# A fused linear attention and two mixtures of experts on one core: the first attention steps in another order, their evictions on VectorE, other planned load times, and early expert results kept in the input tile

## The chip, the cores and the metric

The kernel runs on one core of one Trainium2 chip. The metric is the device time of one execution in microseconds (us). Before the change it is 1239.43 us, the median of three runs (1235.06 to 1243.83).

## What is computed

Attention is a recurrence over 768 tokens for 4 batches of 8 heads with 48 elements each: a 48x48 state per head is read by the query, then corrected by the key and the value.

```python
for t in range(S):
    kt, vt, bt = (k_n[:, :, t], v[:, :, t], beta[:, :, t, None])
    y[:, :, t] = np.einsum('bhd,bhde->bhe', q[:, :, t], state)
    v_old = np.einsum('bhde,bhd->bhe', state, kt)
    state = state + bt[:, :, :, None] * np.einsum('bhd,bhe->bhde', kt, vt - v_old)
```

`k_n` is the key divided by its length. The 3072 rows of 384 elements then pass a first mixture (8 experts, each row to the one with the highest logit, `relu(x @ w1) @ w2`, times two gates) and a second one (4 experts, every row through all, weighted by `domain_probs`).

## The kernel before

**Three phases.** The attention with the routing of its rows (`Attention`, `Router`), the first mixture (`Moe.moe1`) and the second one (`Moe.moe2`) follow each other. Each phase is a list of operations with an engine, an assumed duration, what they read and write, and a priority; `Plan.order` (lines 132 to 188) plays the list through once, always taking the earliest operation that can start and among several the one of the lower priority number, and emits the program in that order. On the chip each engine then keeps strictly to its own order. Assumed durations therefore decide the order, not the time. A DMA is two planned operations: its issue on a queue (`D` is SyncE, `A` ScalarE, `G` GpSimd) and a transfer of `xfer` ns. Where TensorE (PE) has a planned gap, small matmuls of zeros (line 252) are put in.

**Attention.** The tokens of a batch are cut into 12 stages of 64. For each stage `st`: `load` (line 310) fetches keys, queries and values into `kf`, `qf` and `v` (5, 2 and 2 buffers); `keys` (319) transposes them on PE into a bank `pb` and moves that ("evicts" it) to `kqT`; `gram` (333) multiplies keys with keys and queries into `GQ` and collects diagonal blocks in `Dg`; `masks` (350) zeroes a triangle of `GQ` on GpSimd (POOL); `scale` (404) multiplies `v` by the key lengths `nt` on POOL. For each pair of stages `inverse` (359) inverts 16x16 triangles on VectorE (DVE): a transpose to `GZ`, a square root on ScalarE (ACT) into `s1`, small steps that give `nt`, then 29 dependent multiply and add steps on `X` (lines 374 to 376). `turn` (377) transposes `X` to `TN` and `C`, and `finish` (381) completes `C` by two PE products (`prod`, line 398) for each stage. `chain` (410) is the recurrence: `r` (values minus what the state gives), two triangular PE products `tri` into `rw` with an eviction to `w` after each, `up` into `Sp`, and the evictions of `Sp` to the state `Sf`, which the next stage needs.

**Routing and the early window.** `Router.done` routes 128 rows at a time; when 16 of the 24 row groups are placed, `early` (586) counts (`few`), gathers the first rows of experts 0 and 1 through one tile, splits and transposes them into `xe[0]` and `xe[1]`. `window(0)` (612) runs 192 rows of expert 0 while the attention ends: eight products into `h` (lines 624 to 626) and three into `y` (633 to 635), whose results go to `x2` in DRAM. Its tiles `h` and `y` lie in `GQ` buffers that the attention no longer needs. `moe1` begins with `window_` for expert 1 on `xe[1]` (line 815) and with the gathers `xg` of the other rows (802). Its tiles lie where the attention's were, so their first writers wait for what still reads there.

## Time and profile before

| what | before |
|---|---|
| median of three runs | 1239.43 us |
| the profiled execution's own time | 1235.26 us |
| its span, first to last instruction | 1233.7 us |
| busy: PE, DVE, ACT, POOL | 94%, 63%, 50%, 52% of the span |
| attention, up to the first product of `moe1` | 306.1 us |

A row of the trace's order of time gives start (us), duration (us), engine, line, operation, what is written from what, and the count; in brackets stands how long the engine had been idle before, and what released it. PEld is the weight load of a matmul, SPq, ACTq and POOLq are DMA issues. PEclk is the clock that the throttle granted to PE, as a share of 2.4 GHz.

### The profile page before, as it was taken

The page shows a single profiled execution, that of the slowest core. Times are in us where ns is not written, and L with a number is a line of the kernel's source. Part 1 is how long each engine was busy: PE and PEld are TensorE (multiplying, and loading weights), DVE is VectorE, ACT ScalarE, POOL GpSimd, SP SyncE. Part 2 cuts the span into 40 slices and gives each one's busy share as a digit, 9 for nine tenths or more (in the row PEclk, how much of TensorE's full clock was granted, in tenths as well). Part 3 has the DMA queues.
Part 4 walks back from the last instruction along what each step waited for, and adds up shares of the span by engine and source line. Part 5 has one row for each costly group of instructions (what it writes and reads, how often), then busy time and mean ns, then how long its engine had stood idle before and what let it go on. Part 6 is the DMA issues. An engine that isn't in the chain of part 4 may idle for free.

```text
span 1233.7 us, 38757 instructions
## 1 busy us (share of the span) xinstructions
PE 1163.3 (94%) x16595; PEld 1018.3 (83%) x16595; DVE 778.2 (63%) x1583; ACT 619.2 (50%) x1129; POOL 642.0 (52%) x896
## 2 busy tenths in 40 slices
PE   6877888879899999999999999999999999999997
PEld 5876777768765555699999999999999999999997
DVE  3766647664578887166666556676666775555555
ACT  4646665553366666255454444454444554444442
POOL 9733422442573341075556544576544575566665
PEclk9989899989999999999999999999999999999999
DMA  8545442322499996111111111121111110111101
GB/s 136 90 98 119 97 92 58 94 83 69 93 263 240 251 231 199 39 38 40 40 39 40 36 44 44 48 60 51 46 57 49 52 40 27 40 53 52 53 27 40
DMA packets 151458, 100.74 MB, mean 82 GB/s; under 512 B 107697, under 2 KB 140433, under 8 KB 151281
## 3 DMA queue, kind: packets, MB, share of 16 engines
q1 hardware_dynamic: 133520, 69.18, 22.9%
q0 software_dynamic: 9216, 23.50, 6.7%
q10 hardware_dynamic: 8544, 5.53, 1.5%
q8 instruction: 131, 2.15, 0.7%
q14 instruction: 47, 0.38, 0.1%
HBM read 77.09 MB, written 15.77 MB: 75 GB/s over the span
## 4 chain that ended last, share of the span: by engine, by line
PE 57%; DVE 0%; issue 0%; POOL 0%; ACT 0%; POOLq 0%
PE b L956 31%; PE b L975 26%; POOL out_dram L994 0%; DVE h L968 0%; DVE cc L986 0%; DVE wa L990 0%; DVE sm L986 0%; ACT h L967 0%; ACT a L958 0%; POOLq L1052 0%; POOL sep L993 0%; POOLq L994 0%
## 5 line engine op out<-in xcount | busy, mean ns | idle before, releaser
L956 PE MATMUL b<-wb,v 128*128 128x256 f16 x3456 | 392.6, 273 | 0.7 <-PEq L923 0.7
L956 PEld LDWEIGHTS <-v 128*128 128x128 f16 x3456 | 336.7, 98 | 38.1 <-issue 1.1
L975 PE MATMUL b<-v,h 128*128 128x192 f16 x4032 | 348.0, 246 | 0.0
L975 PEld LDWEIGHTS <-h 128*128 128x128 f16 x4032 | 335.5, 98 | 2.2
L964 POOL TENSOR_TENSOR S<-a 128x256 f32<-128x256 f32 x192 | 150.8, 805 | 250.5 <-ACT a L958 250.2
L968 DVE TENSOR_TENSOR h<-a,h 128x768 f16<-128x768 f32 x96 | 133.0, 1386 | 133.2 <-ACT h L967 124.9
L968 DVE TENSOR_TENSOR h<-S,h 128x1024 f16<-128x1024 f32 x96 | 117.6, 1225 | 125.7 <-ACT h L967 125.7
L958 ACT ACTIVATE a<-b 128x512 f32<-128x512 f32 x192 | 113.8, 595 | 151.6 <-PE b L956 149.2
L967 ACT ACTIVATE h<-S 128x1024 f16<-128x1024 f32 x96 | 101.4, 1056 | 161.2 <-POOL S L964 141.5
L964 POOL TENSOR_TENSOR S<-S,a 128x256 f32<-128x256 f32 x96 | 127.0, 1323 | 0.0
L967 ACT ACTIVATE h<-a 128x768 f16<-128x768 f32 x96 | 81.0, 843 | 3.0
L964 POOL TENSOR_TENSOR S<-a,S 128x256 f32<-128x256 f32 x96 | 77.1, 803 | 7.2
L986 DVE TENSOR_TENSOR cc<-b,sm 128x192 f32<-128x192 f32 x192 | 58.7, 347 | 2.4 <-ACT sm L980 2.4
L833 POOL DMA_DIRECT2D x<-y x24 | 17.1, 712 | 61.5 <-DVE y L830 40.3
L818 DVE SCALAR_TENSOR_TENSOR h<-b,h 128x432 f16<-128x432 f32 (+2 forms) x72 | 37.8, 527 | 16.3 <-ACT h L817 16.2
L817 ACT ACTIVATE h<-b 128x432 f16<-128x432 f32 (+2 forms) x72 | 32.9, 466 | 29.5 <-PE b L815 29.0
L986 DVE TENSOR_TENSOR sm<-b,sm 128x192 f32<-128x192 f32 x144 | 46.2, 349 | 1.5
L767 DVE SCALAR_TENSOR_TENSOR v<-s,v 128x512 f16<-128x512 f32 (+2 forms) x56 | 42.6, 775 | 5.9 <-ACT v L766 5.8
L802 POOL DMA_INDIRECT xg<-xd,wid x28 | 30.5, 1088 | 22.8 <-issue 6.6
L269 POOL DMA_DIRECT2D stw<-in_moe_w_dram x28 | 16.0, 572 | 47.8 <-DVE X L376 17.9
L815 PE MATMUL b<-xt,w 128*128 128x432 f16 x216 | 40.2, 346 | 0.2 <-DVE h L818 0.2
L827 PE MATMUL b<-h,w 128*128 128x432 f16 x216 | 39.9, 346 | 0.0
(286 smaller groups left out, 1727.9 us busy)
## 6 DMA issues: line engine op xcount, KB each, us to landing
wb<-x SPq DMA_DIRECT2D x72, 256.0 KB
s<-in_moe_w_dram SPq DMA_DIRECT2D x40, 384.0 KB
s<-in_moe_w_dram SPq DMA_DIRECT2D x18, 512.0 KB
s<-in_moe_w_dram SPq DMA_DIRECT2D x24, 256.0 KB
xd<-ys ACTq DMA_DIRECT2D x24, 192.0 KB
x<-y POOLq DMA_DIRECT2D x18, 216.0 KB
stw<-in_moe_w_dram POOLq DMA_DIRECT2D x12, 256.0 KB
stw<-in_moe_w_dram POOLq DMA_DIRECT2D x16, 192.0 KB
```

The source lines that it names most:

```text
L767: self.op('V',(150+1.042*n)*self.slow,lambda: self.nc.vector.scalar_tensor_tensor(out=lo,in0=s,scalar=64.0,in1=hi,op0=ALU.mult,op1=ALU.sub ...
L815: nc.tensor.matmul(out=ps,lhsT=w1[:,a,k,f*128:(f+1)*128],rhs=xt[:,b*KD+k],start=i==0,stop=i==8); i+=1
L817: self.op('A',160+.85*n,lambda ps=ps,h=h: nc.scalar.activation(out=h[:,0],in_=ps,func=AF.Relu),[('p1',pi)],[('h',hi,0)],**U)
L818: self.op('V',150+1.042*n,lambda ps=ps,h=h: nc.vector.scalar_tensor_tensor(out=h[:,1],in0=ps,scalar=0.0,in1=h[:,0],op0=ALU.max,op1=ALU.sub ...
L827: nc.tensor.matmul(out=ps,lhsT=w2[:,a,f,d*128:(d+1)*128],rhs=hs[f][0][:,b],start=(f,i)==(0,0),stop=(f,i)==(KF-1,2))
L956: for c,y in PASS: nc.tensor.matmul(out=F[k][:,f],lhsT=w[:,c,d,c_:c_+128],rhs=self.xk[B%2][d][:,y,256*i:256*i+256],start=(f,z)==(0,0),stop ...
L958: self.op('A',620,lambda k=k,g=g: A.activation(out=a[ja][:,g].rearrange("p x t -> p (x t)"),in_=F[k].rearrange("p a t -> p (a t)"),func=AF ...
L964: self.op('G',930,lambda o=o,x=x,y=y,w=w: G.tensor_tensor(out=X[o],in0=X[x],in1=X[y],op=w),ka,[ks])
L967: self.op('A',200+.833*m,lambda h=h,q=q,g=g: A.activation(out=h[:,0,:,q],in_=g,func=AF.Copy),kg,[kh+(0,)])
L968: self.op('V',1400 if m==768 else 1350,lambda h=h,q=q,g=g: V.tensor_tensor(out=h[:,1,:,q],in0=g,in1=h[:,0,:,q],op=ALU.subtract),kg+[kh+(0, ...
L975: for z,(c,d) in enumerate(PASS): nc.tensor.matmul(out=Q[k][:,o,0:192],lhsT=h[:,c,g,x],rhs=w[:,d,m,y],start=(m,o,z)==(0,0,0),stop=(m,z)==( ...
L986: self.op('V',340,lambda o=o,k=k,y=y,x=x: V.tensor_tensor(out=o,in0=Q[k][:,y,0:192],in1=s[:,x],op=ALU.add),[(qk,k),('sm',z,x)],[ko])
```

## The change

Eight edits, all but the last two in the first stages of the attention.

1. The load of the square root's table onto ACT and the memset ahead of it move from priority -40 to -61, to the front of both engines.
2. `xfer` of a key, query or value load is 9.4 ns a row for stages 0 and 1, 12 for stages 2 to 4 (`LDX`), and 8.5 as before for the rest.
3. All key evictions of stages 0 and 1 go to DVE (before: one half of the heads on ACT).
4. Of the two evictions of a `gram` of stages 0 and 1 the second goes to DVE.
5. `masks` of stages 0 and 1 get a much earlier priority; those of stage 2 wait for the first state `Sf`.
6. `scale` of stage 0 is gone: `r` of stage 0 is one DVE multiplication of `v` by `nt` (before: a POOL multiplication, then an ACT copy). `scale` of stage 1 waits for `C` of stage 1, that of stage 2 for the first `Sf`.
7. In `window`, `y` is written over `xe`, the window's own input tile, after its last reader.
8. The three DMAs of `y` to `x2` go to SyncE's queue (`YQ`).

```diff
+LDX = 12
+YQ = 'D'
...
-        self.op('V',100,lambda: nc.vector.memset(self.s1,1.0),(),['s1'],"table")
-        self.op('A',1450,lambda: nc.scalar.activation(out=self.s1,in_=self.s1,func=AF.Sqrt),['s1'],['s1'],"table")
+        self.op('V',100,lambda: nc.vector.memset(self.s1,1.0),(),['s1'],"table",prio=-61)
+        self.op('A',1450,lambda: nc.scalar.activation(out=self.s1,in_=self.s1,func=AF.Sqrt),['s1'],['s1'],"table",prio=-61)
...
-                self.dma(d,h[b,:,64*st+x:64*st+x+m].rearrange("h t d -> t h d"),(),[(n,i,b,x)],f"ld {st} {w}",xfer=8.5*m,occ=640 if x in (0,64) and m==64 or x==0 else 490,q=q[b//2%len(q)])
+                self.dma(d,h[b,:,64*st+x:64*st+x+m].rearrange("h t d -> t h d"),(),[(n,i,b,x)],f"ld {st} {w}",xfer=(9.4 if st<2 else LDX if st<5 else 8.5)*m,occ=640 if x in (0,64) and m==64 or x==0 else 490,q=q[b//2%len(q)])
...
-            e='AV'[hh] if st<2 else 'A'; s=lambda P=P: P[0:112,:].rearrange("p (h g t) -> p h g t",h=4,g=2)
+            e='V' if st<2 else 'A'; s=lambda P=P: P[0:112,:].rearrange("p (h g t) -> p h g t",h=4,g=2)
...
-            for t in range(2): self.act(594,GQ[t][:,4*hh:4*hh+4].rearrange("p h i -> p (h i)"),lambda P=P[t]: P[:,:],[ks[t]],[wr[t]],tg,give=[ks[t]])
+            for t in range(2):
+                o=GQ[t][:,4*hh:4*hh+4].rearrange("p h i -> p (h i)")
+                if st<2 and t: self.op('V',690,lambda o=o,P=P[t]: nc.vector.tensor_copy(out=o,in_=P[:,:]),[ks[t]],[wr[t]],tg,give=[ks[t]])
+                else: self.act(594,o,lambda P=P[t]: P[:,:],[ks[t]],[wr[t]],tg,give=[ks[t]])
...
-            self.op('G',1250,lambda P=P,t=t: nc.gpsimd.tensor_tensor(out=P,in0=P,in1=self.mask[t].rearrange("p (o i) -> p o i",o=1).to_broadcast([128,H,64]),op=ALU.mult),['mask']+kg,kg,f"mask {st}",prio=st-0.5)
+            self.op('G',1250,lambda P=P,t=t: nc.gpsimd.tensor_tensor(out=P,in0=P,in1=self.mask[t].rearrange("p (o i) -> p o i",o=1).to_broadcast([128,H,64]),op=ALU.mult),['mask']+kg+([('Sb',0,0)] if st==2 else []),kg,f"mask {st}",prio=st-0.5 if st>1 else -19.5)
...
+        if st==0: return
...
-            self.tt('G',950,v,v,n,ALU.mult,k+[('nt',c%3)],k,f"vn {st}")
+            self.tt('G',950,v,v,n,ALU.mult,k+[('nt',c%3)]+([('C',0,1)] if st==1 else [('Sb',0,0)] if st==2 else []),k,f"vn {st}")
...
-                self.act(470,r[j],v[j],kv,[k0[j]],tg,**U); continue
+                self.op('V',550,lambda j=j: V.tensor_tensor(out=r[j],in0=v[j],in1=self.nt[c%3].rearrange("p (t h s o) -> p h t s o",t=2,s=2,o=1)[:,4*j:4*j+4,:,s].to_broadcast([128,4,2,D]),op=ALU.mult),kv+[('nt',c%3),kc],[k0[j]],tg,prio=-18.5); continue
...
-        hs=U[0:8] if e==0 else U[8:16]; y0=16; s0=8*e; x=self.xe[e]; kx=[('xe',e,j) for j in range(2)]
+        hs=U; s0=0; x=self.xe[e]; kx=[('xe',e,j) for j in range(2)]
...
-            k=('eq',e,d); P=Lazy(at,k); y=U[y0+d]; ky=('ey',e,d)
+            k=('eq',e,d); P=Lazy(at,k); y=x[:,2*d:2*d+2]; ky=('ey',e,d)
...
-            at.dma(self.x2[d][:,:,0:n],y,[ky+(0,),ky+(1,)],[('x2',d)],t,xfer=n*2,q='G')
+            at.dma(self.x2[d][:,:,0:n],y,[ky+(0,),ky+(1,)],[('x2',d)],t,xfer=n*2,q=YQ)
```

The program's order changes in many places. Three are shown.

ACT's queue around the square root of the first inverse (`s1<-GZ`). Key evictions write `wb` and `wa` from `pb` with 112x8x64 (stages 2 and 3), `gram` evictions with 128x512. Before:

```order
L257 ACTIVATE wa_82<-pb0_150 112x8x64 [waits PE_49]
L257 ACTIVATE wa_82<-pb2_152 112x8x64 [waits PE_49]
L257 ACTIVATE wb_83<-pb3_153 128x512 [waits PE_49]
L257 ACTIVATE wa_82<-pb1_151 128x512 [waits PE_49]
L257 ACTIVATE wa_82<-pb0_150 112x8x64 [waits PE_49]
L257 ACTIVATE s1_129<-GZ_119 128x32 [waits DVE_49]
L257 ACTIVATE wa_82<-pb2_152 112x8x64 [waits PE_49]
L257 ACTIVATE wb_83<-pb3_153 128x512 [waits PE_49]
L257 ACTIVATE wa_82<-pb1_151 128x512 [waits PE_49]
L257 ACTIVATE Dg_118<-wb_83,mm_95 128x256 [waits Activation_49]
```

After:

```order
L259 ACTIVATE wb_83<-pb0_150 112x8x64 [waits PE_49]
L259 ACTIVATE wb_83<-pb1_151 112x8x64 [waits PE_49]
L259 ACTIVATE wb_83<-pb2_152 112x8x64 [waits PE_49]
L259 ACTIVATE wb_83<-pb3_153 112x8x64 [waits PE_49]
L259 ACTIVATE s1_129<-GZ_119 128x32 [waits DVE_49]
L259 ACTIVATE wb_83<-pb0_150 128x512 [waits PE_49]
L259 ACTIVATE wa_82<-pb1_151 128x512 [waits PE_49]
L259 ACTIVATE wb_83<-pb2_152 128x512 [waits PE_49]
L259 ACTIVATE wa_82<-pb3_153 128x512 [waits PE_49]
L259 ACTIVATE wa_82<-pb0_150 112x8x64 [waits PE_49]
L259 ACTIVATE wa_82<-pb1_151 112x8x64 [waits PE_49]
L259 ACTIVATE Dg_118<-wb_83,mm_95 128x256 [waits Activation_49]
```

Ahead of the square root stood an eviction of stage 3's queries (the third row of `wa` with 112x8x64, bank `pb0`); after, the last eviction ahead of it is one of stage 2's queries, and those of stage 3 stand behind it.

POOL's queue from the first stage's `finish` to the scaling of `v`; `L2` is an operand of `finish`, `mask0` and `mask1` are the triangles, `row` is a small load. Before:

```order
L391 TENSOR_TENSOR L2_126<-GQ10_112,ml_96 128x16x16 [waits PE_49,Activation_49,Pool_49]
L269 DMA row_70<-in_moe2_domain_probs_dram 32x12x4 [waits DMASW6_49]
L391 TENSOR_TENSOR L2_126<-GQ11_113,ml_96 128x16x16 [waits PE_49,Activation_49,Pool_49]
L354 TENSOR_TENSOR GQ10_112<-GQ10_112,mask0_92 128x8x64
L354 TENSOR_TENSOR GQ11_113<-GQ11_113,mask1_93 128x8x64
L391 TENSOR_TENSOR L2_126<-wb_83,ml_96 128x16x16 [waits PE_49,Activation_49,Pool_49]
L269 DMA row_70<-in_moe2_domain_probs_dram 32x12x4 [waits DMASW7_49]
L391 TENSOR_TENSOR L2_126<-wa_82,ml_96 128x16x16 [waits PE_49,Activation_49,Pool_49]
L260 TENSOR_TENSOR v0_105<-v0_105,nt1_133 128x384 [waits DMAHW1_49,DMAHW4_49,DVE_49,Activation_49]
L260 TENSOR_TENSOR v0_105<-v0_105,nt1_133 128x384 [waits DMAHW5_49,DMAHW6_49,DMAHW3_49,DMAHW2_49]
L354 TENSOR_TENSOR wb_83<-wb_83,mask0_92 128x8x64
L354 TENSOR_TENSOR wa_82<-wa_82,mask1_93 128x8x64
```

After:

```order
L396 TENSOR_TENSOR L2_126<-GQ10_112,ml_96 128x16x16 [waits PE_49,Activation_49,Pool_49]
L271 DMA row_70<-in_moe2_domain_probs_dram 32x12x4 [waits DMASW6_49]
L359 TENSOR_TENSOR GQ10_112<-GQ10_112,mask0_92 128x8x64
L396 TENSOR_TENSOR L2_126<-GQ11_113,ml_96 128x16x16 [waits PE_49,Pool_49]
L271 DMA row_70<-in_moe2_domain_probs_dram 32x12x4 [waits DMASW7_49]
L359 TENSOR_TENSOR GQ11_113<-GQ11_113,mask1_93 128x8x64
L396 TENSOR_TENSOR L2_126<-wb_83,ml_96 128x16x16 [waits PE_49,Activation_49,Pool_49]
L271 DMA row_70<-in_moe2_domain_probs_dram 32x12x4 [waits DMASW0_49]
L396 TENSOR_TENSOR L2_126<-wa_82,ml_96 128x16x16 [waits PE_49,Activation_49,Pool_49]
L271 DMA row_70<-in_moe2_domain_probs_dram 32x12x4 [waits DMASW1_49]
L271 DMA row_70<-in_moe2_domain_probs_dram 32x12x4 [waits DMASW2_49]
L262 TENSOR_TENSOR v1_106<-v1_106,nt0_132 128x384 x2
```

The masks of stage 2 (`wb`, `wa`) and the scaling of `v0` by `nt1` stood right behind `finish`; after, they are further down the queue, and the two masks of stage 1 have a DMA between them. The masks of stage 0 stand further ahead in the queue.

ACT's queue where the attention ends: `ys` is the output of the last stage, `GZ<-GZ,sc` a split of gathered rows for the early window, `GQ30` to `GQ31` at line 626 (632 after the change) the first products of that window. Before:

```order
L257 ACTIVATE w0_137<-rw0_147 128x384 [waits DVE_49,PE_49]
L583 ACTIVATE GZ_119<-GZ_119,sc_79 128x384 [waits DMAHW2_49,DMASW3_49,DVE_49]
L626 ACTIVATE GQ30_114<-pb3_153 128x192 [waits PE_49]
L257 ACTIVATE w1_138<-rw1_148 128x384 [waits PE_49,Activation_49]
L257 ACTIVATE xT_158<-pb0_150 128x384 [waits PE_49,Activation_49]
L257 ACTIVATE ys1_141<-pb1_151 128x4x2x48 [waits DMAHW5_49,DMAHW4_49,PE_49]
L257 ACTIVATE ys1_141<-pb2_152 128x4x2x48 [waits PE_49]
L269 DMA xd_57<-ys1_141 128x384 [waits Activation_49]
L269 DMA xd_57<-ys1_141 128x384
L626 ACTIVATE GQ30_114<-pb3_153 128x192 [waits PE_49]
L257 ACTIVATE xT_158<-pb1_151 128x384 [waits PE_49]
```

After:

```order
L589 ACTIVATE GZ_119<-GZ_119,sc_79 128x384 [waits DMASW0_49,DVE_49]
L259 ACTIVATE w0_137<-rw0_147 128x384 [waits PE_49,Activation_49]
L259 ACTIVATE xT_158<-pb1_151 128x384 [waits PE_49]
L259 ACTIVATE w1_138<-rw1_148 128x384 [waits DVE_49,PE_49]
L259 ACTIVATE ys1_141<-pb2_152 128x4x2x48 [waits DMAHW5_49,DMAHW4_49,PE_49]
L259 ACTIVATE ys1_141<-pb3_153 128x4x2x48 [waits PE_49]
L271 DMA xd_57<-ys1_141 128x384 [waits DMAHW1_49,Activation_49]
L271 DMA xd_57<-ys1_141 128x384 [waits DMAHW2_49]
L589 ACTIVATE GZ_119<-GZ_119,sc_79 128x384 [waits DMAHW0_49,DMASW1_49,DVE_49]
L259 ACTIVATE xT_158<-pb0_150 128x384 [waits PE_49]
L259 ACTIVATE xT_158<-pb2_152 128x384 [waits PE_49,Activation_49]
L259 ACTIVATE xT_158<-pb1_151 128x384 [waits PE_49,Activation_49]
```

Before, the last of the four splits and two evictions of the early window (one of them further up) stood ahead of the last `ys`; after, one split does, and three splits and the whole window follow. On DVE, the last transposition to `TN` stood 23 rows behind the state eviction of stage 9 (rows 448 and 425); after, it stands 8 rows ahead of it (434 and 442). The eleven state evictions on DVE stand at rows 101, 124, 163, 199, 258, 278, 316, 351, 387, 425 and 475 before, at 109, 135, 171, 211, 267, 295, 348, 366, 412, 442 and 472 after.

## Rows read from the trace of the kernel before

**Rows 1.** Chain of waits by line, and stretches with busy times, clock, DMA.

```profile
by line: PE b L956 30.6%; PE b L975 26.1%; issue 0.4%; POOL out_dram L994 0.2%; DVE h L968 0.2%; DVE cc L986 0.1%; DVE wa L990 0.1%; DVE sm L986 0.1%; ACT h L967 0.1%; ACT a L958 0.0%; POOL sep L993 0.0%; POOLq L1052 0.0%; POOLq L994 0.0%
...
core 0: us, PE busy (x) PEld busy (x) DVE busy (x) ACT busy (x) POOL busy (x), PEclk, DMA share, GB/s
52.00:74.00 22.00, 16.85 (x601) 15.17 (x602) 18.00 (x37) 7.19 (x20) 14.94 (x20) 0.69 0.26 58
74.00:292.50 218.50, 183.37 (x6414) 160.34 (x6415) 137.26 (x390) 132.10 (x307) 77.40 (x110) 0.95 0.40 94
...
516.00:1233.00 717.00, 709.97 (x7488) 670.55 (x7486) 436.07 (x685) 333.88 (x492) 417.51 (x481) 1.00 0.15 45
```

**Rows 2.** Order of time, 0 to 14 us: first evictions and first gram.

```profile
8.11 0.69 DVE L331 COPY kqT<-pb 112x512 f32<-112x512 f32 x1 [1.34 <-PE pb L326]
...
11.29 0.60 ACT L257 ACTIVATE kqT<-pb 112x512 f32<-112x512 f32 x1
...
13.97 1.10 PE L341 MATMUL pb<-kqT 48*64 48x128 f32 x32 [2.27 <-ACT kqT L257]
```

**Rows 3.** Order of time, 27 to 43 us: the first inverse begins.

```profile
27.15 1.98 DVE L362 STREAM_TRANSPOSE GZ<-Dg 128x1024 f32<-128x1024 f32 x1
...
31.88 1.71 PE L326 MATMUL pb<-idv,qf 128*112 128x128 f32 x8 [2.89 <-DMA qf<-in_q_dram]
...
33.55 0.18 DVE L365 TENSOR_SCALAR s<-s 128x32 f32<-128x32 f32 x1 [4.42 <-ACT s L257]
...
37.07 0.78 DVE L348 SCALAR_TENSOR_TENSOR Dg<-wb,mm,Dg 128x256 f32<-128x256 f32 x1 [1.78 <-ACT Dg L257]
...
42.20 0.52 ACT L257 ACTIVATE Dg<-GQ,mm 128x256 f32<-128x256 f32 x1
```

**Rows 4.** Order of time, 48 to 64 us: turn, finish and POOL beside them.

```profile
48.99 1.11 DVE L379 STREAM_TRANSPOSE TN<-X 128x512 f32<-128x512 f32 x1
...
54.07 1.16 PE L398 MATMUL pb<-MT,NE 64*64 64x64 f32 x64
...
54.88 3.08 DVE L366 TENSOR_TENSOR s<-s,GZ 128x32 f32<-128x32 f32 x1
...
55.39 2.49 POOL L354 TENSOR_TENSOR GQ<-GQ,mask 128x512 f32<-128x512 f32 x2
...
57.88 0.27 DVE L402 TENSOR_TENSOR C<-C,pb 128x128 f32<-128x128 f32 x1
...
59.67 4.16 DVE L368 TENSOR_TENSOR s<-s,bz 128x32 f32<-128x32 f32 x1
```

**Rows 5.** Order of time: first product and state of stage 0, then of stage 9.

```profile
58.85 1.02 PE L412 MATMUL rw<-r,C 32*32 32x48 f32 x60 [0.36 <-DVE C L402]
...
73.08 0.48 ACT L257 ACTIVATE Sf<-Sp 48x384 f32<-48x384 f32 x1 [1.30 <-PE Sp L412]
...
241.01 0.54 PE L412 MATMUL rw<-r,C 32*32 32x48 f32 x32
...
250.38 0.48 ACT L257 ACTIVATE Sf<-Sp 48x384 f32<-48x384 f32 x1
```

**Rows 6.** Order of time, 256 to 310 us: end of attention, start of first mixture.

```profile
256.19 0.17 DVE L590 TENSOR_SCALAR few<-pb 128x8 f32<-128x8 f32 x1 [0.45 <-PE pb L589]
256.35 1.09 DVE L379 STREAM_TRANSPOSE TN<-X 128x512 f32<-128x512 f32 x1
...
279.35 0.48 ACT L257 ACTIVATE Sf<-Sp 48x384 f32<-48x384 f32 x1 [0.37 <-PE Sp L412]
...
290.20 1.21 SPq L269 DMA_TRANSPOSE xe<-GZ  x1
...
306.14 2.40 PE L815 MATMUL b<-xe,wa 128*128 128x192 f16 x27 [0.76 <-DVE GQ L618]
...
308.90 0.78 ACT L817 ACTIVATE h<-b 128x192 f16<-128x192 f32 x3 [3.25 <-PE b L815]
...
309.54 1.03 POOL L802 DMA_INDIRECT xg<-xd,wid  x1 [2.48 <-PE b L815]
```

More of the change, by code (lines that the diff above doesn't have):

```diff
@@ L615, in window @@
         kw=[[(z,e,0,a,x) for z in ('W','W2') for a in range(KD) for x in range(0,FF,512)],[(z,e,1,a,0) for z in ('W','W2') for a in range(KF)]]
-        U=[x.rearrange("p h i -> p (h i)").bitcast(F16)[:,2*n*j:2*n*j+2*n].rearrange("p (a t) -> p a t",a=2) for i in (3,4) for x in at.GQ[i] for j in range(5)]; free=lambda s: [('GQ',3+s//10,hh,s//5%2) for hh in range(2)]
-        hs=U[0:8] if e==0 else U[8:16]; y0=16; s0=8*e; x=self.xe[e]; kx=[('xe',e,j) for j in range(2)]
+        U=[x.rearrange("p h i -> p (h i)").bitcast(F16)[:,2*n*j:2*n*j+2*n].rearrange("p (a t) -> p a t",a=2) for i in (3,4) for x in at.GQ[i] for j in range(5)][0:8]; free=lambda s: [('GQ',3+s//10,hh,s//5%2) for hh in range(2)]
+        hs=U; s0=0; x=self.xe[e]; kx=[('xe',e,j) for j in range(2)]
         def lo(q,k,o,reads,wr,give,op0,sc): at.op('V',150+1.042*n,lambda: nc.vector.scalar_tensor_tensor(out=o[:,1],in0=q(),scalar=sc,in1=o[:,0],op0=op0,op1=ALU.subtract),reads,wr,t,give=give)
@@ L634, in window @@
                 at.op('P',6*(n/2.4+3),mm,[('eh',e,f,j) for f in (f0,f0+1) for j in range(2)]+kw[1],[k],t,take=[k] if f0==0 else (),lat=LP,ni=12)
-            at.op('A',160+.85*n,lambda P=P,y=y: nc.scalar.activation(out=y[:,0],in_=P[:,0:n],func=AF.Copy,scale=2.0**-8),[k],[ky+(0,)],t,after=free(y0+d))
+            at.op('A',160+.85*n,lambda P=P,y=y: nc.scalar.activation(out=y[:,0],in_=P[:,0:n],func=AF.Copy,scale=2.0**-8),[k],[ky+(0,)],t,after=kx)
             lo(lambda P=P: P[:,0:n],k,y,[k,ky+(0,)],[ky+(1,)],[k],ALU.mult,2.0**-8)
-            at.dma(self.x2[d][:,:,0:n],y,[ky+(0,),ky+(1,)],[('x2',d)],t,xfer=n*2,q='G')
+            at.dma(self.x2[d][:,:,0:n],y,[ky+(0,),ky+(1,)],[('x2',d)],t,xfer=n*2,q=YQ)
     def counts(self):
```

## The prediction, made before the changed kernel ran

> **What bounds the kernel now.** I read the chain of waits first. It ends in the second mixture: two PE lines hold 57% of the span, and in the stretch from 516 us on PE is busy for 710 of 717 us [rows 1]. Nothing of the change is in there, so it can only move the start of that stretch. The table of stretches then says where room is: in the attention (the first 306 us) no engine is full; from 74 to 292.5 us PE is busy 84% (with its fillers), DVE 63%, DMA 40% [rows 1]. That part is bound by latency, by who waits for whom in a fixed order, and I read it in the order of time, up to the first state, at the last stages, and where the first mixture takes over. I assume that what the attention ends earlier arrives at the end: the first mixture behind it depends on nothing else that has a time of its own.
>
> **The first inverse.** DVE has the inverse's transpose done at 27.15 + 1.98 = 29.13 us and sits idle until 33.55, since the square root stands on ACT behind an eviction of stage 3's queries, whose load comes so late that PE begins their transposes at 31.88 [rows 3]. The new ACT order has them behind the square root, so 33.55 - 29.13 = 4.4 us go. What takes their place: behind 31.88 ACT still has two evictions of those queries, four of their grams, two of stage 4's keys and two `Dg`, and DVE needs the second `Dg` inside its 29 steps. Ten ACT operations of 0.5 to 0.6 us after a transpose of 1.7 end near 31.9 + 1.7 + 8 x 0.57 + 2 x 0.5 = 39.2 (estimate from [rows 2, 3]; before the first of these `Dg` was at 42.20). Behind it DVE has twelve of the 29 steps. These and what prepares them took 48.99 - 37.85 = 11.1 us [rows 3, 4], of which four operations for `Dg` took about 0.5 each, so twelve steps take at most 12/29 x 9.1 = 3.8 us, and `TN` would start near 43.0 where it now starts at 48.99. That is 6 us. If that load binds harder (it lands 2 us later, and a transpose stands idle) 3 remain; if not at all, everything ahead of 33.55 and the wait of 1.78 at 37.07 [rows 3] also counts, some 10. I take 6: the late load is in the trace, and the change doesn't issue it earlier.
>
> **Evictions and the table.** Eight evictions move to DVE at 0.69 us where ACT took 0.60 [rows 2], +0.7 us in all; DVE is idle there (1.34 us before the first). The first gram waited 2.27 us for ACT at 13.97 [rows 2], which that ends. The table load now stands between ACT's first and second DMA issue and makes its ten other loads later by its own time, 1.45 us as the plan assumes it (no row of the trace shows it apart). Both lie ahead of 29.13 and are covered by the late load above: taken as nothing, -1.5 to +4 if that cover is gone.
>
> **POOL against DVE.** A DVE operation of 32 columns, 0.18 us at 33.55 [rows 3], takes 3.08 us at 54.88 and 4.16 us at 59.67, and both end as POOL's run of masks and scalings ends [rows 4]. Queued behind the first is the update of `C` at 57.88, although its product was ready at 55.2; the first triangular product waits for it. After the change POOL has DMA issues between these operations, so one operation of about 1.25 us may still hold DVE, not three: 1.5 us gained of 2.9 (0 to 2.9). The second stands in the way of stage 0's chain. From the first product to the state, stage 0 takes 73.08 - 58.85 = 14.2 us, stage 9 takes 250.38 - 241.01 = 9.4 [rows 5]; the granted clock also falls there, to a mean of 0.69 over 52 to 74 us [rows 1]. With masks and scalings of stage 2 moved behind the state I take the 4.8 us difference, less 2 x 0.55 us for `r` (384 columns, from the 0.69 us for 512 [rows 2]), which now stands on DVE between the update and the product: 3.7 (1 to 6). The Trainium skill speaks against it: by "SBUF — State Buffer", section "Who interferes with whom", a VectorE instruction with two SBUF inputs is held by a GpSimd instruction that reads SBUF until that has ended. The two long rows agree. By that rule the new `r` can be held as they were, and an eviction out of PSUM cannot.
>
> **The middle.** `r`, evictions and masks are done after stage 2; stages 2 to 10 keep their work, but not their order. The inverse runs further ahead: counting DVE's rows, the state evictions of stages 6 to 9 have 15 to 32 more rows ahead of them, 10 of which are the moved evictions and `r`; that of stage 10 has 3 fewer. DVE passed one instruction per 218.5 / 390 = 0.56 us there [rows 1]. So stage 6 could come 22 x 0.56 = 12.3 us later against the shifted time, and stage 10, which now waits for the `TN` at 256.35 (its state at 279.35, 29 us after stage 9's) [rows 5, 6], 13 x 0.56 = 7.3 us earlier. Only the last counts for the end. I take 4, half of it, since a count is no time (bounds -8 to +8).
>
> **The end.** From stage 10's state to the first product of `moe1` it takes 306.14 - 279.35 = 26.8 us. The gathers for the early window begin with `few` at 256.19 and end with the last transpose at 290.20 + 1.21: 35.2 us [rows 6], of waits for the tile that they share. In the new order `few` stands behind the second product of stage 10, some 5 us ahead of that state, so `xe[1]` is ready 30.4 us after it: 3.6 us lost (0 to 7). That also covers the window's three products that no longer run ahead of the last stage. Then ACT's first eviction in `moe1` waited 3.25 us, to 308.90, and the first gather to 309.54, 2.4 to 3 us after they could have started: their tiles lay on the `y` that POOL's DMA still read [rows 6]. With `y` in `xe` that wait goes: 2.5 us (0 to 3.5). SyncE's queue has nothing ahead of these three DMAs but the rows' own, and its transposes for `moe1` come later.
>
> **The sum.** 6 + 1.5 + 3.7 + 4 - 3.6 + 2.5 = 14.1 us. The profiled execution took 1235.26 us, of which the span is 1233.7; it becomes 1221.2. It lay 4.2 below the median of the three runs, so the median to expect is 1239.4 - 14.1 = 1225.3, rounded to 1225, 1.2% less. About 1% (12.4 us) is what a measurement of this kernel can tell from no change.
>
> **Rivals.** *The late load holds.* Stage 3's queries bind the inverse harder (3 instead of 6) and nothing is won in the middle: 3 + 1.5 + 3.7 - 3.6 + 2.5 = 7.1, 1232 us. For it: DVE already waits for ACT at 37.07 as well [rows 3]. Against it: ACT has fewer evictions ahead. *The lock comes back.* `r` meets stage 1's second mask, and the postponed masks and scalings of stage 2 hold the second inverse's steps for as long as the longer of these rows, 4.2 us: 14.1 - 5.2 - 4.2 = 4.7, 1235 us. For it: the two long rows [rows 4]; against it: DMA issues stand between some of them. This is the skill's rule above, as a mechanism. *The inverse pushes the chain,* and the time gets longer: the 12.3 us at stage 6 are real and not won back, so -12.3 stands for +4: 6 + 1.5 + 3.7 - 12.3 - 3.6 + 2.5 = -2.2, 1242 us. It turns the sign from a push of 10.1 us on. For it: DVE is the engine of both, in a fixed order. Against it: the present gap of 29 us ahead of stage 10 shows that stages are waiting for inverses, not the other way round. That the change would do nothing is hard to see, since the new order has the square root free.
>
> **Chances.** Forecast 0.58 (its own range 1217 to 1233), late load 0.2, lock 0.1, push 0.12. The forecast's bounds put some two thirds of it below 1227, which is 1% less; the two middle cases add little there, and one in ten of each. So faster by over 1%: 0.47. Slower by over 1% needs the push and hardly any gain at the start: 0.07. Within 1%: 0.46. For 8 in 10 the range reaches over the late load and the lock to the push, and down to the forecast with 10 us at the inverse and 8 in the middle: 1212 to 1242.
>
> **What would show it.** `TN` first at 41 to 44 us and the square root right behind `GZ`, with the wait moved to a `Dg`; the two long DVE rows gone or under 1.5 us; first state at 60 to 63 us; stage 10's state within 17 us of stage 9's, near 264 us; the first product of `moe1` near 294, ACT's eviction under 1 us behind it. I am wrong if the first state comes early and the last does not: then the order in the middle decides, not the start. If the first state comes after 68 us, it is the loads or the lock.

## The result, and the profile after

The changed kernel takes 1225.74 us (median of 8 runs, 1224.34 to 1229.97), the kernel before 1236.98 us beside it (1233.62 to 1245.85). The ratio is 0.9915, with a 95% interval of 0.9888 to 0.9942: 11.2 us by the medians. Measured once more (after_again, below) it took 1229.93 us against 1237.2, ratio 0.9929 (0.9905 to 0.9952). The forecast was 1225 us and 14.1 us less; 1225 is what came, but three of the six terms that made it up were off by more than 4 us, and they cancelled.

The profiled execution of the changed kernel took 1225.39 us, its span is 1223.7 us. The chain that ended last, by engine, and three stretches (the columns are those of [rows 1]):

```profile
PE 75%; DMA 7%; issue 7%; DVE 5%; POOL 2%; ACT 2%; SPq 1%; ACTq 0%; POOLq 0%; DVEq 0%
...
43.00:67.00 24.00, 18.15 (x699) 16.54 (x693) 19.08 (x38) 11.88 (x32) 15.30 (x21) 0.93 0.47 91
67.00:265.00 198.00, 168.48 (x6006) 148.63 (x6004) 139.53 (x364) 124.03 (x290) 75.53 (x104) 0.95 0.42 94
505.00:1223.00 718.00, 710.52 (x7490) 670.70 (x7488) 435.72 (x685) 334.89 (x493) 415.27 (x481) 1.00 0.15 45
```

The second mixture is what it was: 718 us with PE busy for 710.5, where [rows 1] had 717 and 710. All that moved lies ahead of it.

The first inverse, order of time (the answer to [rows 3]):

```profile
19.58 1.94 DVE L367 STREAM_TRANSPOSE GZ<-Dg 128x1024 f32<-128x1024 f32 x1
22.45 1.58 DVE L370 TENSOR_SCALAR s<-s 128x32 f32<-128x32 f32 x1 [0.93 <-ACT s L259]
24.45 1.99 DVE L371 TENSOR_TENSOR s<-s,GZ 128x32 f32<-128x32 f32 x1
...
34.93 1.93 PE L328 MATMUL pb<-idv,kf 128*112 128x128 f32 x8 [3.05 <-DMA kf<-in_k_dram]
36.04 0.60 ACT L259 ACTIVATE kqT<-pb 112x512 f32<-112x512 f32 x1 [3.14 <-PE pb L328]
37.38 0.90 ACT L259 ACTIVATE Dg<-GQ,mm 128x256 f32<-128x256 f32 x2
37.91 0.48 DVE L353 SCALAR_TENSOR_TENSOR Dg<-GQ,mm,Dg 128x256 f32<-128x256 f32 x1 [3.82 <-ACT Dg L259]
...
42.25 1.14 DVE L384 STREAM_TRANSPOSE TN<-X 128x512 f32<-128x512 f32 x1
```

The square root follows `GZ` at once (0.93 us of idle time instead of 4.42). Inside the 29 steps there is a new wait of 3.82 us: ACT has the `Dg` of stage 3 behind the evictions of stage 4's keys, whose load PE got at 34.93. `TN` starts at 42.25 instead of 48.99.

From there to the first state (the answer to [rows 4, 5]):

```profile
46.81 1.16 PE L403 MATMUL pb<-C,L 64*64 64x64 f32 x64
...
49.35 1.29 POOL L359 TENSOR_TENSOR GQ<-GQ,mask 128x512 f32<-128x512 f32 x1
49.62 1.07 DVE L370 TENSOR_SCALAR s<-s 128x32 f32<-128x32 f32 x1 [2.67 <-ACT s L259]
50.99 2.41 DVE L353 SCALAR_TENSOR_TENSOR Dg<-GQ,mm,Dg 128x256 f32<-128x256 f32 x1
51.81 1.27 POOL L359 TENSOR_TENSOR GQ<-GQ,mask 128x512 f32<-128x512 f32 x1
53.87 0.28 DVE L407 TENSOR_TENSOR C<-C,pb 128x128 f32<-128x128 f32 x1
55.71 1.01 DVE L442 TENSOR_TENSOR r<-v,nt 128x384 f32<-128x384 f32 x2
56.31 1.01 PE L418 MATMUL rw<-r,C 32*32 32x48 f32 x64 [3.90 <-DVE r L442]
...
66.61 0.48 ACT L259 ACTIVATE Sf<-Sp 48x384 f32<-48x384 f32 x1 [2.63 <-PE Sp L418]
67.12 0.56 DVE L457 COPY Sf<-Sp 48x384 f32<-48x384 f32 x1 [1.72 <-ACT Sf L259]
```

Two `Dg` operations of one shape take 0.48 us at 37.91 and 2.41 us at 50.99; the long one ends 0.3 us behind POOL's mask of 51.81. PE waits 3.90 us for `r`. From `TN` to stage 0's first product (56.31 us) it is 14.1 us, where it was 9.9 (48.99 to 58.85); from there to ACT's eviction to `Sf` it is 10.3 us (66.61), where it was 14.2.

The end of the attention (the answer to [rows 6]):

```profile
235.69 1.08 DVE L384 STREAM_TRANSPOSE TN<-X 128x512 f32<-128x512 f32 x1
241.25 0.56 DVE L457 COPY Sf<-Sp 48x384 f32<-48x384 f32 x1 [1.49 <-PE Sp L418]
258.97 0.16 DVE L596 TENSOR_SCALAR few<-pb 128x8 f32<-128x8 f32 x1
264.98 0.56 DVE L457 COPY Sf<-Sp 48x384 f32<-48x384 f32 x1 [3.40 <-ACT Sf L259]
275.85 0.49 ACT L259 ACTIVATE ys<-pb 128x384 f32<-128x384 f32 x1 [0.44 <-PE pb L418]
283.82 2.75 PE L630 MATMUL pb<-xe,kq 128*128 128x192 f16 x18
288.11 7.93 SPq L271 DMA_TRANSPOSE xe<-GZ  x2
298.77 1.00 POOL L808 DMA_INDIRECT xg<-xd,wid  x1 [3.82 <-ACT xe L641]
298.92 3.29 PE L821 MATMUL b<-xe,wa 128*128 128x192 f16 x38 [0.89 <-DVE xe L624]
299.91 0.33 ACT L823 ACTIVATE h<-b 128x192 f16<-128x192 f32 x1 [1.51 <-PE b L821]
```

The last `TN` starts 20.7 us earlier than in [rows 6], stage 10's state 14.9 us earlier (DVE's copy: 279.9 before), the first product of `moe1` only 7.2 us earlier; ACT's eviction follows it by 1.0 us, and the first gather stands 0.15 us ahead of it.

### The profile page after: what moved, and what is told of

It reads as the page before. It is cut to its first block, busy times and chain, and to the rows that moved or that the text cites. A ratio compares the mean times of both kernels' runs of the same rounds, so it can differ in the third digit from the quotient of the medians.

```text
span 1223.7 us, 38674 instructions
## 1 busy us (share of the span) xinstructions
PE 1158.0 (95%) x16552; PEld 1015.2 (83%) x16552; DVE 795.6 (65%) x1593; ACT 615.2 (50%) x1118; POOL 635.9 (52%) x891
## 4 chain that ended last, share of the span: by engine, by line
PE 75%; DMA 7%; issue 7%; DVE 5%; POOL 2%; ACT 2%; SPq 1%; ACTq 0%; POOLq 0%; DVEq 0%
PE b L962 30%; PE b L981 26%; PE b L821 4%; PE b L833 3%; PE pb L418 2%; PE rw L418 2%; PE pb L328 2%; DMA x<-y 1%; PE pb L403 1%; DMA xt<-xh 1%; SPq L271 1%; PE pb L343 1%; DMA s<-in_moe_w_dram 1%; DMA kf<-in_k_dram 1%; PE Sp L418 1%
## 5 line engine op out<-in xcount | busy, mean ns | idle before, releaser
L839 POOL DMA_DIRECT2D x<-y x24 | 17.2, 715 | 62.4 <-DVE y L836 42.9
L824 DVE SCALAR_TENSOR_TENSOR h<-b,h 128x432 f16<-128x432 f32 (+2 forms) x72 | 37.9, 528 | 13.5 <-ACT h L823 13.1
L823 ACT ACTIVATE h<-b 128x432 f16<-128x432 f32 (+2 forms) x72 | 33.2, 466 | 23.8 <-PE b L821 23.6
L262 POOL TENSOR_TENSOR v<-v,nt 128x384 f32<-128x384 f32 x22 | 18.8, 864 | 39.9 <-DMA v<-in_v_dram 29.9
```

Source lines behind the costliest of these rows:

```text
L824: self.op('V',150+1.042*n,lambda ps=ps,h=h: nc.vector.scalar_tensor_tensor(out=h[:,1],in0=ps,scalar=0.0,in1=h[:,0],op0=ALU.max,op1=ALU.sub ...
```

## The experiments

All times below are medians, with the ratio to the kernel before on the same chip. "State" is DVE's copy to `Sf` of a stage; the last one is stage 10's. The fourth column is the time from stage 6's state to the last `GZ`; all other columns but the last two are starts in the profiled execution, in us.

| kernel | first TN | first state | stage 6 to last GZ | last TN | last state | moe1 starts | time | ratio (95%) |
|---|---|---|---|---|---|---|---|---|
| before | 49.0 | 73.6 | 23.9 | 256.4 | 279.9 | 306.1 | 1237.0 | |
| changed | 42.3 | 67.1 | 14.6 | 235.7 | 265.0 | 298.9 | 1225.7 | 0.9915 (0.9888 to 0.9942) |
| after_again | 42.7 | 67.9 | 14.8 | 237.6 | 265.8 | 302.2 | 1229.9 | 0.9929 (0.9905 to 0.9952) |
| win_old | 41.3 | 66.0 | 14.1 | 237.9 | 267.6 | 301.8 | 1232.7 | 0.9940 (0.9916 to 0.9963) |
| dg3_first | 38.4 | 68.2 | 14.9 | 238.9 | 268.7 | 303.7 | 1231.0 | 0.9928 (0.9903 to 0.9953) |
| r_early | 41.2 | 67.9 | 14.6 | 237.2 | 266.3 | 301.0 | 1232.8 | 0.9954 (0.9929 to 0.9980) |
| mask_late | 42.1 | 68.2 | 14.0 | 237.9 | 267.1 | 301.6 | 1233.4 | 0.9950 (0.9926 to 0.9973) |
| mask_dve | 42.9 | 65.6 | 15.0 | 235.3 | 263.4 | 299.9 | 1229.0 | 0.9938 (0.9914 to 0.9961) |
| gather2 | 43.0 | 66.4 | 14.8 | 234.1 | 261.6 | 297.0 | 1231.2 | 0.9956 (0.9935 to 0.9977) |
| evict_swap | 42.6 | 66.2 | 14.4 | 231.6 | 260.9 | 295.7 | 1229.6 | 0.9907 (0.9878 to 0.9935) |
| evict_old | 43.5 | 67.8 | 29.5 | 257.1 | 279.4 | 308.2 | 1241.4 | 1.0041 (1.0013 to 1.0068) |
| ldx_old | 43.9 | 67.2 | 25.7 | 256.6 | 286.9 | 313.7 | 1246.2 | 1.0051 (1.0020 to 1.0081) |
| load14 | 47.0 | 72.1 | 18.5 | 250.1 | 278.3 | 313.6 | 1238.8 | 0.9980 (0.9957 to 1.0002) |
| win_only | 48.7 | 73.2 | 23.8 | 261.0 | 285.1 | 311.2 | 1239.3 | 1.0002 (0.9967 to 1.0036) |

**after_again** is the changed kernel once more. 

> The changed kernel itself, so that the one-move kernels have it on their chip. If what win_old, dg3_first, r_early and mask_late cost more than it (1231 to 1233 us against 1225.7) is the moves, it takes 1225 to 1227 us here. If it is the chip and the scatter of its loads, it takes 1229 to 1232, and no one-move kernel differs from it by more than 3 us.

It took 1229.93 us. The kernels with one move lie at 1229.0 to 1233.4, within 3.5 us of it: no move in them is shown to be worth more than the scatter. The last state is at 265.8 us against 265.0, but from `moe1`'s first product to the second mixture's it took 212.7 us against 206.5, with 7.0 us of PE waits for `h` there against 2.2. Over the nine profiled executions with the changed order this stretch is 206 to 216 us long.

### The start: does it pass through?

**dg3_first** takes away the new wait.

```diff
 # emitted order, ACT alone
+move(ACT: Dg of stage 3, ahead of the first eviction of stage 4's keys)
```

> The changed kernel with one move on ACT alone: the two Dg operations of stage 3 stand ahead of the two evictions of stage 4's keys, which wait for a load. Every theory expects that DVE's wait of 3.82 us ahead of 37.91 goes and the first TN starts near 38.4 instead of 42.25. Theory A (the start of the inverse is what the first state waits for): first state 3.8 us earlier, near 63.3, and the time about 1222. Theory B (PE still transposes stage 4's queries, which come by load, in its own order ahead of the first product of finish, to 45.6): that product at 45.6 to 46.8 as now, first state at most 1.2 us earlier, time within 1.5 us of 1225.7.

The first `TN` started at 38.42 us, as expected, but the first product of `finish` only at 45.87 (46.81 in the changed kernel); the first state came at 68.2, later than without the move, and the time is that of after_again. Theory B holds at the start, and more: nothing of the 3.8 us is left at the first state.

**r_early** and **mask_late** each move two operations.

```diff
 # r_early: emitted order, DVE alone
+move(DVE: the two r of stage 0, behind the second GZ transpose)
 # mask_late: emitted order, POOL alone
+move(POOL: the two masks of stage 1, behind the scaling of v1)
```

> The changed kernel with one move on DVE alone: the two r of stage 0, which need only v and nt, stand right behind the second GZ transpose, where DVE is idle for 2.7 us, instead of behind the update of C. Theory of the lock and of r as its price: the first triangular product starts at 54.6 instead of 56.31, the first state 1.7 us earlier, near 65.4; if the start passes through, the time is 1.7 us less, 1224.0. Rival (loads and PE's own stalls set the middle): first state earlier, stage 5 and later ones within 0.5 us of now, time within 1 us of 1225.7.

> The changed kernel with one move on POOL alone: the two masks of stage 1 stand behind the scaling of v1 instead of between the operands of finish. Theory of the lock (POOL's masks still hold DVE between 49.6 and 54.4 us): the Dg operation of 2.41 us at 50.99 falls to 0.5 to 0.9, the one of 1.07 us ahead of it to 0.2, the first update of C comes at 51.5 to 52.2 instead of 53.87, the first triangular product near 54 instead of 56.31, first state 2 to 3 us earlier. Rival (the update waits for PE and ACT, the long DVE rows only fill the wait): update within 0.5 us of 53.87, first state unchanged. For the time: 2 to 3 us less if the start passes through, within 1 us if the middle absorbs it.

In r_early the first triangular product started at 52.5 us, in mask_late at 51.0 (56.3 in the changed kernel), so the lock and `r` did hold it. Yet the first states came at 67.9 and 68.2. The hold had moved. In r_early, DVE and POOL in order of time:

```profile
47.30 3.96 DVE L370 TENSOR_SCALAR s<-s 128x32 f32<-128x32 f32 x1
47.43 1.29 POOL L359 TENSOR_TENSOR GQ<-GQ,mask 128x512 f32<-128x512 f32 x1
...
48.67 0.62 POOL L396 TENSOR_TENSOR L<-GQ,ml 128x256 f32<-128x256 f32 x1
...
49.23 0.64 POOL L271 DMA_DIRECT2D row<-in_moe_domain_probs_dram  x1
...
49.88 1.28 POOL L359 TENSOR_TENSOR GQ<-GQ,mask 128x512 f32<-128x512 f32 x1
```

One small DVE operation lasts until 51.26, the end of the second mask at 51.16, through four POOL rows of which one is a DMA issue. Further on POOL runs stage 2's scaling and masks from 57.8 to 61.9, ahead of the state for which edits 5 and 6 let them wait: that wait is one of the plan, which the chip does not know, and with `v` free earlier its load came earlier (SyncE issues it from 49.51 us in r_early, from 56.75 in the changed kernel). In mask_late a DVE step of 2.59 us stands at 59.90 and the second `r` behind it, at 62.41; PE waits 2.87 us for it, and the granted clock is 0.50 (1.2 GHz) from 56 to 68 us. In r_early it is 0.57 on average from 60 to 68 us. So less came of the earlier product for more reasons than the hold.

**mask_dve** takes POOL's masks away.

```diff
-nc.gpsimd.tensor_tensor(out=P,in0=P,in1=self.mask[t]...,op=ALU.mult)
+(nc.vector if st in (1,2) else nc.gpsimd).tensor_tensor(out=P,in0=P,in1=self.mask[t]...,op=ALU.mult)
 # emitted order
+move(DVE: the masks of stages 1 and 2, behind DVE's copy to the first state)
```

> The changed kernel with the four masks of stages 1 and 2 on DVE instead of POOL, right behind DVE's copy to the first state: no mask of POOL can hold DVE ahead of it. Theory of the lock: no DVE row of 128x32 between 47 and 60 us over 1.0 us but beside POOL's scaling of v, first triangular product near 51 to 52, first state 3 us or more ahead of 67.1, near 63. Rival (loads, the code fetches of PE and its clock set the first state): still 66 to 68. For the time: 3 us less than the changed kernel on this chip if the start passes through; within 1.5 us if the loads of the middle absorb it.

First product at 52.2 us, no DVE row of the inverse over 1.03 us between 47 and 60. The first state came at 65.6, 22.6 us behind its `TN` where the changed kernel takes 24.9: some 2 us, not 4 or 5, and the time (1229.0) does not show them. The first product is 4.1 us earlier than in the changed kernel; behind it PE stands 4.69 us in three waits for which the profile shows no cause (1.83 in the changed kernel), which the last section takes up.

### What decides: the order in the middle

**evict_old** undoes edits 3 and 4.

```diff
-e='V' if st<2 else 'A'
+e='AV'[hh] if st<2 else 'A'
...
-if st<2 and t: self.op('V',690,...
+if False: self.op('V',690,...
```

> The changed kernel with edits 3 and 4 undone (one half of the key evictions of stages 0 and 1 and all gram evictions on ACT), the order planned anew. The prediction took these edits as nothing, since the late load covers all ahead of 29.13 us. If that holds: the first GZ later than 19.6, but the first TN within 1.5 us of 42.3 and the time within 1.5 us of the changed kernel. Rival (the early evictions are what brought GZ from 27.2 to 19.6, and with it TN): GZ at 24 to 27, TN 3 us or more later, first state 3 us later.

The start is what taking these edits at nothing makes of it: `TN` 43.5, first state 67.8, 0.7 us later. The time is 1241.4 us. All of the gain and more was lost between 68 us and 279 us, with work that the edit does not touch.

**evict_swap** has the same evictions on ACT, in the changed kernel's order.

```diff
-self.op('V',600,... nc.vector.tensor_copy(out=o,in_=s()) ...
+self.op('V',600,... nc.scalar.activation(out=o,in_=s(),func=AF.Copy) if hh==0 else nc.vector.tensor_copy(...) ...
-self.op('V',690,... nc.vector.tensor_copy(out=o,in_=P[:,:]) ...
+self.op('V',690,... nc.scalar.activation(out=o,in_=P[:,:],func=AF.Copy) ...
```

> The changed kernel's order to the row, on every engine, but the evictions of edits 3 and 4 run on ACT at the places where they stand. Against evict_old, in which the same evictions on ACT let the whole order be planned anew (first TN 43.5 us, last TN 257.1, last state 279.4, 1241 us). Theory O (the order of the middle decides: last TN ahead of stage 9's state or behind it): first TN within 3 us of 42.7, last TN at 235 to 241, last state 264 to 270, time 1227 to 1233. Theory E (the engine of these evictions decides): last state 275 or later and time 1238 or more.

Its DVE, in order of time:

```profile
26.14 1.90 DVE L367 STREAM_TRANSPOSE GZ<-Dg 128x1024 f32<-128x1024 f32 x1
42.56 1.17 DVE L384 STREAM_TRANSPOSE TN<-X 128x512 f32<-128x512 f32 x1
231.62 1.11 DVE L384 STREAM_TRANSPOSE TN<-X 128x512 f32<-128x512 f32 x1
260.93 0.56 DVE L457 COPY Sf<-Sp 48x384 f32<-48x384 f32 x1 [3.19 <-ACT Sf L259]
```

The first `GZ` comes 6.6 us later than in the changed kernel, `TN` does not, and the time is that of after_again. So edits 3 and 4 are worth nothing as work moved between engines; what they are worth is the order that the plan makes with them.

**ldx_old** undoes edit 2.

```diff
-...xfer=(9.4 if st<2 else LDX if st<5 else 8.5)*m...
+...xfer=8.5*m...
```

> The changed kernel with edit 2 alone undone (8.5 ns a row for every load); evictions, masks, r and table load as changed. In its order the last TN stands 15 rows behind stage 9's state on DVE, as in the kernel before (23 behind), where the changed kernel has it 8 rows ahead. Theory O (that place decides): first TN and first state as in the changed kernel (42 to 44 and 66 to 69 us), but last TN near 255, last state 276 to 282, time 1235 to 1241. Theory S of the prediction (what the first stages win arrives at the end): last state 265 to 270, time within 2 us of 1230.

Same first state (67.2), and 1246.2 us: theory O was right in direction, and its ranges for the last state and the time were exceeded. With edit 2 nothing changes but planned durations, so the order alone makes this difference. Rows of PE in ldx_old, where stage 11's `gram` (L343) is made (`rw<-Sf` is the first product of the next stage of the recurrence), and two of its DVE at the end:

```profile
211.01 1.10 PE L343 MATMUL pb<-kqT 48*64 48x128 f32 x32
214.70 1.08 PE L418 MATMUL Sp<-w,kf 64*48 64x64 f32 x62
218.31 0.88 PE L418 MATMUL rw<-Sf,wa 112*64 112x96 f32 x16
219.12 1.10 PE L343 MATMUL pb<-kqT 48*64 48x128 f32 x32
...
256.61 1.16 DVE L384 STREAM_TRANSPOSE TN<-X 128x512 f32<-128x512 f32 x1
286.86 0.56 DVE L457 COPY Sf<-Sp 48x384 f32<-48x384 f32 x1 [1.10 <-ACT Sf L259]
```

The same place in the changed kernel:

```profile
201.68 1.98 PE L343 MATMUL pb<-kqT 48*64 48x128 f32 x64
204.54 1.54 PE L418 MATMUL pb<-Sf,wb 112*64 112x96 f32 x32
```

And in the kernel before:

```profile
214.14 1.04 PE L341 MATMUL pb<-kqT 48*64 48x128 f32 x30
...
218.40 1.15 PE L341 MATMUL pb<-kqT 48*64 48x128 f32 x32
```

In the changed kernel both halves of the `gram` stand together, 2 us behind the keys. In ldx_old the second half stands on PE behind the product `rw<-Sf` of stage 8, which needs stage 7's state: the last inverse then starts one stage of the recurrence later. The kernel before, win_only and evict_old have it split in the same way, and the table shows it: 24 to 30 us from stage 6's state to the last `GZ`, 14 to 15 in every kernel with the changed order. Stage 10 follows the last `TN` by 22 to 30 us in all fourteen.

The split is not the whole of that difference. The second half starts 4.3 us behind the first in the kernel before, 8.1 in ldx_old and 10.6 in evict_old, where the fourth column is 9.2, 11.1 and 14.8 us longer than in the changed kernel. Nor is the last inverse the whole of ldx_old's loss: its state of stage 5 comes at 174.95 us, no earlier than in the kernel before (174.62; changed 168.47), and that is ahead of this `gram`. What delays it there no run shows. evict_old is still 7.2 us ahead of the kernel before at stage 8 (229.8 against 237.0) and loses that at stages 9 and 10.

**load14** asks whether the place of the last `TN` alone is enough, with one number in the kernel before.

```diff
-...xfer=8.5*m...
+...xfer=(9.4 if st<2 else 14 if st<5 else 8.5)*m...
```

> The kernel before with one edit, the planned load times: 9.4 ns a row for stages 0 and 1 and 14 for stages 2 to 4 (edit 2 with 14 instead of 12). Evictions, masks, scale, r, table load and the early window are those of before. In its order the last TN stands 8 rows ahead of stage 9's state, as in the changed kernel. Theory O: last TN near 240, last state 265 to 272, time 1228 to 1233 with nothing else of the change. Theory S: no more than the first state gains, 3 us at most, so 1234 or more.

It is not: 1238.8 us. Theory O missed in all its numbers, and theory S's 1234 or more is what came. The `gram` is whole (18.5 us to the last `GZ`), but stage 6's state is at 202.4 us (192.2 in the changed kernel), so that the last `TN` comes at 250.1; `few` came at 272.3 us (259.0), and `moe1` started 35 us behind the last state. A row's place in a queue is not yet its time.

### The end

**win_old** is the changed kernel without edits 7 and 8, **win_only** the kernel before with them alone.

```diff
 # win_old (win_only: the reverse)
-YQ = 'D'
+YQ = 'G'
...
-...y=x[:,2*d:2*d+2]...
+...y=U[y0+d]...
...
```

> The changed kernel with edits 7 and 8 undone: y of the early window in the freed GQ tiles again, its three DMAs on POOL's queue. Nothing ahead of 292 us changes in any engine's order. Theory of the prediction (y in the input tile frees moe1's first tiles): the first eviction of moe1 and the first gather xg, at 299.9 and 298.8 us in the changed kernel, come 2.5 to 3 us later (near 302.5), and the time is 2.5 us more, about 1228. Rival (the end of the changed kernel is set by the gathers for xe[1], which land at 296.0, and the y are hidden): eviction and gather within 0.7 us of where they are, time within 1 us of 1225.7.

> The kernel before with edits 7 and 8 alone (y of the early window in its input tile, its DMAs on SyncE's queue). Nothing ahead of 302 us changes. By the prediction's term moe1's first eviction waits 1 us instead of 3.25, the first gather xg comes within 1 us of the first product instead of 3.4 behind it, and the time is 2.5 us less (1234.5 to 1235.5 where the kernel before takes 1237.5). Rival (hidden, as the gathers of the other rows set the main window): first product of the main window still 18 us behind the first product of moe1, time within 1 us of before.

The start of `moe1` in win_old, order of time:

```profile
301.75 2.39 PE L821 MATMUL b<-xe,wa 128*128 128x192 f16 x27 [0.81 <-DVE GQ L624]
304.48 0.78 ACT L823 ACTIVATE h<-b 128x192 f16<-128x192 f32 x3 [3.17 <-PE b L821]
305.07 1.03 POOL L808 DMA_INDIRECT xg<-xd,wid  x1 [2.39 <-PE b L821]
```

With `y` in the freed tiles ACT and the gather come 2.7 and 3.3 us behind the first product, with `y` in the input tile ACT comes 1.0 us behind it and the gather 0.15 ahead. The main window's first product is 17.8 us behind `moe1`'s in win_old and 13.2 in the changed kernel (13.1 to 15.3 in the other kernels made from it), but 17.2 in win_only (18.1 before). In the time it can't be told from nothing: win_old 0.9940 against 0.9929 and 0.9915, win_only 1.0002, with intervals that overlap.

**gather2** gives the gathers of the early window a second tile.

```diff
-o=self.xge
+gz=(at.GZ...,at.Dg...)[j]; o=gz[:,0:XW]; xh=gz[:,XW:XW+DM]...
```

> The changed kernel with a second tile for the early window's gathers (in Dg, which the attention no longer needs): gathers alternate between two tiles, so the second need not wait until the first is split and transposed. Nothing ahead of 259 us changes. Theory (the four gathers through one tile set the end: 266.84 to 296.0 us, 29 us in the changed kernel): the four gathers take 16 to 20 us instead of 29, xe[1] is there near 286, the first product of moe1 starts 4 to 8 us earlier, and the time is 4 us less than that of the changed kernel on the same chip. Rival (the last rows of the attention, their routing and the early window's own products set it): xe[1] comes early, but the first product of moe1 within 1.5 us of 298.9, time within 1 us.

```profile
278.65 4.48 PE L630 MATMUL pb<-xe,kq 128*128 128x192 f16 x27 [4.38 <-DMA xe<-Dg]
...
283.24 1.22 SPq L271 DMA_TRANSPOSE xe<-Dg  x1
...
296.95 6.10 PE L821 MATMUL b<-xe,wa 128*128 128x192 f16 x72 [0.93 <-DVE xe L624]
```

The last transposition to `xe[1]` leaves its queue at 284.5 us instead of 296.0, and `moe1` still starts 35.4 us behind the last state (33.9 in the changed kernel). The gathers to `xe[1]` do not set the end; the rival won. By the rows the early window does: its products begin at 278.65, where PE has waited 4.38 us for `xe[0]` (283.82 in the changed kernel), and `moe1`'s first product comes 0.93 us behind DVE's last `xe` of that window. Behind this wait the granted clock is 0.50 (1.2 GHz) to 283.1 us, and 27 of the window's products take 4.48 us where 27 take 2.40 in the changed kernel (from 286.95), so 2 us of an earlier window went there. The window was not moved alone.

## Why the prediction was right, and where its steps were not

The number came out 0.7 us from the measured median. Against the sum, on the profiled executions; the 1.1 us for `r`, which the prediction took off the stretch behind the first product, stand in the stretch ahead of it, where `r` ran:

| term | forecast | measured |
|---|---|---|
| first `TN` | 6 | 6.7 |
| lock and `r`: first `TN` to stage 0's first product | 1.5 - 1.1 | -4.2 |
| from there to the first state | 4.8 | 3.9 |
| middle, first to last state | 4 | 8.4 |
| last state to `moe1`'s first product | -3.6 | -7.7 |
| from there to the main window's first product | 2.5 | 4.9 |
| from there to the second mixture | 0 | -1.6 |

1. *The first inverse* was right in place and size: the square root free, the wait moved to a `Dg`, `TN` at 42.25 where 43.0 was said. The cover it named was not quite the one: stage 3's queries no longer held it, stage 4's keys did, which the same count had in it. (One slip in that count: three `Dg` operations, not four, stand in the stretch of 11.1 us, so twelve steps come to 4.0 us, not 3.8.) dg3_first shows that this `TN` is not what the first state waits for.

2. *Evictions taken at nothing* is right as work (evict_swap: `GZ` 6.6 us later, nothing behind it later) and wrong as an edit: without them the plan makes another order, and evict_old is 11.5 us slower than after_again. The prediction priced the instructions that an edit moves and left out what else the order does with it.

3. *The lock* is the step that failed. From `TN` to stage 0's first product it took 14.1 us where it was 9.9: 4.2 lost where 0.4 was to be won. Ahead of that product DVE had one long row, of 3.08 us; now it has three, of 1.07, 2.41 and 1.42 us. The update of `C` starts 11.6 us behind `TN` (8.9 before), and both `r` stand behind it. "DMA issues between these operations" was the reason for one hold instead of three, and r_early shows a hold of 3.96 us that goes on through two masks, what stands between them and a DMA issue. A part is PE's: with stage 4's `gram`, its transposes of queries and fillers ahead of it, the first product of `finish` starts 4.6 us behind `TN` (3.0 before), and dg3_first, with `TN` 3.8 us earlier, moves it by 0.9. The rival "the lock comes back" had 0.1; its mechanism is what happened ahead of the first state, without its second price. The other half of this step held: from the first product to the state 3.9 us were won of 4.8, with a granted clock of 0.93 over 43 to 67 us where it was 0.69 over 52 to 74. By the Trainium skill, "SBUF — State Buffer", section "Who interferes with whom", a VectorE instruction with two SBUF inputs is held by a GpSimd instruction that reads SBUF, and `tensor_scalar` can be held too, in a mode that takes both ports. The rows agree: the `Dg` operation of 2.41 us has two SBUF inputs, the `TENSOR_SCALAR` of 1.07, 1.58 and 3.96 us one. In which mode these ran no row shows.

4. *The middle* was the decisive term and got half of a count of rows. The count was no guide: by it stage 6 could come 12.3 us later against the shifted time, and it came 2.1 us earlier (200.73 to 192.16, where the first state won 6.5). ldx_old, with the same first state, is 16.6 us slower than evict_swap on the same chip. The sentence "I am wrong if the first state comes early and the last does not: then the order in the middle decides, not the start" describes ldx_old and evict_old to the word. That the start passes through, on which the whole sum stood, did not hold there: their first states are 6 us ahead of the kernel before, their times 0.4 and 0.5% behind it.

5. *The end* was lost twice over (-7.7), and not for the reason given: gather2 has `xe[1]` 11.5 us earlier and gains nothing. The window's eleven products and the routing of the last rows now run behind the last `ys`, 23.1 us to `moe1` (298.92 - 275.85) where it was 14.1 (306.1 - 292.0). The prediction had counted the three products that no longer run ahead as covered by the gathers.

6. *The start of `moe1`* came as described: ACT's wait 1.0 us instead of 2.8 and the gather with the first product. It is 4.9 us at the main window, and 1.6 of it are gone at the second mixture. The 3.2 us that are left can't be told from scatter. The assumption that the first mixture "depends on nothing else that has a time of its own" does not hold: the stretch from `moe1`'s first product to the second mixture is 206 to 216 us long in the nine kernels with the changed order (209.7 before), with a DMA share of 1.07 and 1.03 between 350 and 400 us in the two profiles of the changed kernel.

So the number is better than the sum, and that is luck. The terms came to 10.4 us where 14.1 were forecast: 4.6 missing at the lock, 0.9 behind it, 4.1 at the end and 1.6 in the first mixture, against 4.4 more in the middle, 2.4 at the start of `moe1` and 0.7 at the first `TN`. The profiled execution took 1225.39 us where 1221.2 was forecast for it. The median agrees because the forecast started from the median of three runs, 1239.43 us, 4.2 above the profiled execution: eight runs of that kernel give 1236.98, from which the same 14.1 us lead to 1222.9, and the median of the changed kernel lies only 0.4 above its own profiled execution.

Of the signs that were named, `TN` (42.25 us) and ACT's eviction (1.0 us behind) came as said. The first state came at 67.1 us (60 to 63 said), stage 10's 23.7 us behind stage 9's (17 at most), `moe1` at 298.9 us (near 294), and one long DVE row of 2.41 us stayed.

Of the rivals, "the inverse pushes the chain" (0.12) did not come in the changed kernel, where the last inverse starts 17.8 us earlier (224.6 to 206.8); something like it is what evict_old and ldx_old show, where a later last `TN` goes with it, and not a count of rows ahead of the states.

What stays open: what the split `gram` of stage 11 costs by itself. That it goes with the 9 to 15 us of the fourth column was read from rows (split in four kernels, whole in the changed kernel, evict_swap and load14); it was not moved alone. That the order decides, and not the work that edits 3 and 4 move, is shown by evict_swap and ldx_old; which place in it does so is not. Nor was it tried whether the kernel before, with its own evictions and the changed order of the middle alone, is as fast as the changed one. No kernel here is shown to be faster than the changed one; evict_swap and mask_dve are level with it.
